# Order and pace of the weight preparation behind an attention stage

## The chip, the core and the metric

The kernel runs on one core of one Trainium2 chip. The metric is the device time of one execution in microseconds (us). Three executions of the kernel before took 1023.18, 1025.66 and 1025.5 us; the median is 1025.5 us. Engines are named as in the profile: PE is TensorE's matmul, PEld its weight load, DVE is VectorE, ACT ScalarE, POOL GpSimd, SP SyncE.

## What is computed

Three stages follow one another. All inputs are 64-bit floats; the kernel reads them as pairs of 32-bit words, and the three feed-forward weights of the first layer are turned into 32-bit floats on the chip.

```python
# attention: 4 batches, 8 heads, 576 positions, 64 wide, window of 128
scores = scale * q @ k.T ; scores = where(0 <= i - j < 128, scores - slope_h * |i - j|, -1e9)
attn   = exp(scores - max) ; attn /= sum(attn) + 1e-9 ; x = attn @ v      # x: 2304 x 512
# first layer, 512 -> 1536 -> 512
x = (silu(x @ w_gate) * (x @ w_val)) @ w_out
# second layer, 512 -> 2048 -> 512
h = x @ w_in ; out = (h * cos(h)) @ w_out2
```

## The kernel before

**Exactness.** A matrix product of the two layers is made of three matmuls: each operand is split into a high and a low half (`hi`, `lo`), and `mm3` (L79 to L82) adds high by high, high by low and low by high. Splitting an operand takes a copy (high) and a subtraction (low).

**Attention stage (L713 to L791).** A unit is one batch and one pair of heads; there are 16 units. A unit has nine items (four query blocks for each of two heads, and one item for the 64 tail rows of both heads), so the stage runs over 144 items and ten more turns to drain. The loop counter is `n`; unit u has the items 9u to 9u+8. In each turn the loop issues one step of the software pipeline for several items: scores (`do_s`), one turn later the bias (`do_bias`, DVE), two turns later the exponential (`do_exp`, ACT), then the normalising multiply (`do_norm`, POOL), transposes (`do_t`, PE), copies to high and low halves (`do_hi` ACT, `do_lo` DVE), and the product with v (`do_pv`). At fixed places in a unit the q and k of the next unit are transposed into the one buffer `pq` (`prep_t`, L426), read from there (`prep_q`, `prep_k`), and loaded for the unit after (`load_qk`, `load_v`, on SP's queue). The tail rows of q and k are transposed once in each unit, in the turn in which `n` is 4 more than a multiple of nine (L462).

**Batch 0 is different.** Units 0 to 3 (`exact(u)`, items 0 to 35) multiply plain 32-bit floats and need no halves of q and k. From item 36 on, products use halves: more instructions on ACT, DVE and POOL in each unit.

**Filler.** `filler()` (L284) issues first-layer matmuls for three of the twelve column blocks of the hidden width, in between the items, at 1.6 steps a turn (`RATE`). It can begin with a batch when that batch's attention output is complete: for batch 0 that is `release(0)`, in turn n = 45. A job is half a batch of tokens (288 columns): twelve steps with the gate weights, twelve with the value weights, and twelve with the output weights, the latter behind the next job's gate steps. When a job's third gate block has been taken out of PSUM, ACT applies Silu to all three (L236); Silu and the exponential need different tables, so ACT loads a table before and one after (1283 ns each in the trace).

**The filler's weights.** `g0_todo` (L190 to L195) lists nine pieces of 128 by 512: gate, value and output for the three blocks. `convert(..., act=True)` (L99) is a generator that prepares them. One `next(pieces)` is one step of it. A piece takes four or five steps: load of the next piece (512 KB, SP's queue) and a first ACT operation (L122); a second ACT operation (L124) and one on DVE (L125); two on DVE (L132, L133); for pieces of odd number an addition on DVE (L137), for even ones on POOL (L142). Then the high half comes from ACT (L164, even pieces) or POOL (L169, odd pieces), the low half from POOL (L157). The POOL operations go through the queue `pool_bg`, from which each turn takes about one unit of cost, and through `post`, which is emptied in the next turn. Two pieces take nine turns. A matmul step of the filler isn't issued until its piece is entered in `g0`; the generator waits in turn for older pieces.

Every engine runs its instructions in the order of issue. The list scheduler is not used (`manual_schedule`): the program order written here is the order on each queue.

Of the kernel before, what the change touches and what calls it, by code (L numbers as in the profile page):

```python
# [28 lines left out]
def kernel(  # L29
# [17 lines left out]
    NP = H // 2  # L47
# [5 lines left out]
    NI = 2 * NB + 1  # L53
# [129 lines left out]
    F0 = 3  # L183
# [5 lines left out]

    g0_todo = []  # L190
    pools0 = [wa_p, wa_p, wa2_p]
    for f in range(F0):
        g0_todo.append((("g", f), w_gate, f, True, pools0[f]))
        g0_todo.append((("v", f), w_val, f, True, pools0[f]))
    g0_todo += [(("o", f), w_out, f, False, pools0[f]) for f in range(F0)]  # L195

    def flush():
# [107 lines left out]
    def run_fill(n):  # L305
        done = 0
        while done < n and alive[0]:
            r = next(fill, None)
            if r == "wait":
                break  # L310
            if r == "end":
                alive[0] = False
                break
            done += 1
        return done
# [106 lines left out]
    def prep_t(u, nm, pool=None):  # L422
        t = nat[nm, u]
        ps = pool.tile([128, 512], F32, tag="t", name="t") if pool else ps_q.tile([128, 512], F32, tag="pq", name="pq")
        for i in range(NB):
            nc.tensor.transpose(ps[:, i * 128:(i + 1) * 128], t[:, i].rearrange("p h d -> p (h d)"), ident)  # L426
        PQ[u, nm] = ps
# [33 lines left out]
    def prep_tail_t(u, ps):  # L461
        nc.tensor.transpose(ps[:, 384:512], nat["t", u].rearrange("p h d -> p (h d)"), ident)  # L462
        PQ[u, "t"] = ps[:, 384:512]
# [30 lines left out]
    def prep_vh(u):  # L494
        if NP <= u < NP + 2:
            vhl[u % 2] = big.tile([128, NB, 4, D], F32R, tag=f"vhl{u % 2}", name=f"vhl{u % 2}")
        nc.gpsimd.tensor_scalar(v_part(u, 0), nat["v", u], 1.0, 0.0, ALU.mult, ALU.add)
# [9 lines left out]
    for u in range(U):  # L507
# [4 lines left out]
        for j in range(0, NI, 2):  # L512
            g = list(range(u * NI + j, u * NI + min(j + 2, NI)))
# [13 lines left out]
    def do_s(g):  # L527
        ps = ps_s.tile([128, 512], F32, tag="s", name="s")
        st = s_p.tile([128, 8], F32, tag="st", name="st")
        at = 0  # L530
        for m, n in enumerate(g):
            u, h, i = items[n]
            w = width(i)
            o = ps[:, at:at + w]
            at += w
            if i == NB:
                a = tail_q(u)
                c = slice(S - w, S)
                product(u, o, a, KT[u], slice(0, 128), slice(0, 128), c)
            else:  # L540
                qc = slice(i * 128, (i + 1) * 128)
                c = slice((i + 1) * 128 - w, (i + 1) * 128)
                if exact(u):
                    product(u, o, QT[u], KT[u], slice(64 * h, 64 * h + 64), qc, c)
                else:
                    product(u, o, [x[:, h] for x in QT[u]], KT[u], slice(0, 128), qc, c)
            SP[n] = o
            ST[n] = st, m

    def do_bias(n):  # L550
        u, h, i = items[n]
        w = width(i)
        p = u % NP
        e = e_p.tile([128, 256], F32, tag="e", name="e")
        st, m = ST[n]
        nc.vector.tensor_tensor_reduce(  # L556
            out=e[:, :w], in0=SP.pop(n), in1=relt if i == NB else rel[:, 256 - w:],
            scale=slope[:, p:p + 1] if i == NB else slopes[2 * p + h], scalar=3.0e38,
            op0=ALU.add, op1=ALU.min, accum_out=st[:, m:m + 1])
        E[n] = e  # L560

    def do_exp(n):
        w = width(items[n][2])
        e, (st, m) = E[n], ST[n]
        nc.scalar.activation(out=e[:, :w], in_=e[:, :w], func=AF.Exp, bias=st[:, m:m + 1], scale=-1.0,  # L565
                             accum_out=st[:, 2 + m:3 + m])

    def do_guard(g):
        st = ST[g[0]][0]
        c = len(g)  # L570
        nc.vector.tensor_scalar(st[:, 4:4 + c], st[:, 2:2 + c], 1e-9, None, ALU.add)

    def do_recip(g):
        st = ST[g[0]][0]
        c = len(g)
        nc.vector.reciprocal(out=st[:, 6:6 + c], in_=st[:, 4:4 + c])  # L576

    def do_norm(n):
        w = width(items[n][2])
        (st, m), e = ST.pop(n), E[n]  # L580
        nc.gpsimd.tensor_scalar(e[:, :w], e[:, :w], st[:, 6 + m:7 + m], 1.0, ALU.mult, ALU.mult)  # L581

    def do_t(g):
        ps = ps_t.tile([128, 512], F32, tag="t", name="t")
        at = 0
        for n in g:
            w = width(items[n][2])
            e = E.pop(n)
            for j in range((w + 127) // 128):
                c = min(j * 128, w - 128)  # L590
                nc.tensor.transpose(ps[:, at:at + 128], e[:, c:c + 128], ident)  # L591
                at += 128
        PT[g[0]] = ps[:, :at]
        TT[g[0]] = ps
# [5 lines left out]
    def do_hi(g):  # L600
        ps = PT[g[0]]
        if items[g[0]][2] == NB:
            nc.scalar.copy(out=ptt, in_=ps)
        else:
            u, h, i = items[g[0]]
            if u == NP and i == 0:
                pth[h] = big.tile([128, NB * 256 - 128], F32R, tag=f"pth{h}", name=f"pth{h}")
            nc.scalar.copy(out=pth[h][:, split_cols(g)], in_=ps)

    def do_lo(g):  # L610
        ps = PT.pop(g[0])
        if items[g[0]][2] < NB and not exact(items[g[0]][0]):
            c = split_cols(g)
            u, h, i = items[g[0]]
            if u == NP and i == 0:
                ptl[h] = big.tile([128, NB * 256 - 128], F32R, tag=f"ptl{h}", name=f"ptl{h}")
            nc.vector.tensor_tensor(out=ptl[h][:, c], in0=ps, in1=f32(pth[h][:, c]), op=ALU.subtract)
# [95 lines left out]
    CONV0, RATE = 4, 1.6  # L713
# [3 lines left out]
    for n in range(N + PVS + 1):  # L717
        due += 0.7 * RATE
        u, idx = divmod(n, NI)
        v1 = u + 1 if u + 1 < U else None  # L720

        def ended(j):
            return final.get(n - j)

        todo = list(post)
        post.clear()
        if n in first:
            do_s(first[n])
        if ended(LOW):
            do_lo(ended(LOW))  # L730
        if ended(HIGH):
            do_hi(ended(HIGH))
        for m in first.get(n - EXP, ()):
            do_exp(m)
        for m in first.get(n - 1, ()):
            do_bias(m)
        if ended(NORM):
            do_guard(ended(NORM))
        if ended(TRANS):
            do_t(ended(TRANS))  # L740
        if v1 is not None:
            if idx == TT0:
                g = ended(TRANS)
                prep_tail_t(v1, TT[g[0]] if g else ps_t.tile([128, 512], F32, tag="t", name="t"))
        if ended(NORM):
            do_recip(ended(NORM))
            for m in ended(NORM):
                do_norm(m)
        for fn in todo:
            fn()  # L750
        due -= run_fill(int(due))
        due += 0.3 * RATE
        for back in (PVS + 1, PVS):
            g = ended(back)
            if g:
                u_, h_, i_ = items[g[0]]
                if (back > PVS) == (u_ >= NP and h_ == 1 and i_ == 0):
                    for m in g:
                        do_pv(m)
        if v1 is not None:  # L760
            if idx == Q0 + 1:
                prep_q(v1)
            if idx == Q0:
                prep_t(v1, "q")
            if idx == K0:
                prep_t(v1, "k")
            if idx == K0 + 1:
                prep_k(v1)
            if idx == TT0 + 1:
                prep_tail(v1)  # L770
            if idx == max(TT0, K0) + 1:
                load_qk(u + 2)
            if idx == 7:
                load_v(u + 1)
        if u < U:
            if idx == 2:
                prep_vh(u)
            elif idx in (3, 4):
                prep_vl(u, idx - 3)
        pdue = min(pdue + 1.0, 1.0)  # L780
        while pool_bg and pdue > 0:
            cost, fn = pool_bg.popleft()
            fn()
            pdue -= cost
        if n < 8:
            t, h = qz[n // 4][n // 2 % 2], n % 2
            nc.gpsimd.memset(f32(t[64 - 64 * h:128 - 64 * h, h]), 0.0)
        if n >= CONV0:
            next(pieces, None)
        due = min(due - run_fill(int(due)), RATE)  # L790
    settle()  # L791
# [286 lines left out]
    i, tb, f = steps[0]  # L1078
# [26 lines left out]
    for k in range(K + 1):  # L1105
        if k < K:
            i, tb, f = steps[k]
# [226 lines left out]
```

## Time and profile before

| | |
|---|---|
| three timed executions | 1023.18, 1025.66, 1025.5 us; median 1025.5 |
| the profiled execution | 1027.21 us; span from the first to the last instruction 1025.4 us |
| PE busy, share of the span | 997.0 us, 97% |
| ACT, DVE, POOL busy | 648.9, 765.1, 512.6 us |
| chain that ended last, by engine | PE 88%, ACT 6% |
| mean granted clock of TensorE in the span | 0.992 |

The profiled execution is 1.7 us above the median of the timed ones. A busy PE is not always PE at its peak: the duration of a matmul of the same shape tells which of its two clocks (1.2 and 2.4 GHz) it ran at, and the column of the granted clock tells it where the recorder saw a change.

### The profile page before, as it was taken

To read this page: it belongs to the slowest core of one execution; us is meant where nothing else is said; L and a number is where in the kernel's file an instruction comes from. 1 tells how busy PE (TensorE), PEld (TensorE's weight loads), DVE (VectorE), ACT (ScalarE), POOL (GpSimd) and SP (SyncE) were. 2 spreads that over 40 slices of the span, in tenths; PEclk is the share of its full clock that TensorE was granted. 3 is DMA by queue.
4 is the path that set the end of the run, shared out by engine and by line. 5 is a ranking of instruction groups with operands and counts; after the bars stand their busy time and mean duration, and the time that the engine had idled before them with its cause. 6 is when DMAs were issued, how large, how long until landed. Compare 5 with 4: busy or idle time off the path is not lost.

```text
span 1025.4 us, 17616 instructions
## 1 busy us (share of the span) xinstructions
PE 997.0 (97%) x5796; PEld 938.7 (92%) x5796; DVE 765.1 (75%) x1600; ACT 648.9 (63%) x1438; POOL 512.6 (50%) x585
## 2 busy tenths in 40 slices
PE   7989999999999999999999999899999999999998
PEld 5778999999999999999999999798899988999986
DVE  5897797786419898998989944869866797656664
ACT  5888889887315454555545532867768777677663
POOL 5776676575315666866867840324323343222231
PEclk9989999999999999999999999999999999999999
DMA  6542333322246464755846651956667556575552
GB/s 150 135 120 48 71 85 76 80 54 66 67 159 237 124 195 127 246 162 165 266 125 212 200 175 62 312 184 202 218 199 259 167 195 195 169 260 177 184 177 82
DMA packets 145164, 163.69 MB, mean 160 GB/s; under 512 B 64689, under 2 KB 105649, under 8 KB 144817
## 3 DMA queue, kind: packets, MB, share of 16 engines
q1 hardware_dynamic: 145072, 162.57, 51.1%
q8 instruction: 46, 0.75, 0.3%
q14 instruction: 46, 0.37, 0.1%
HBM read 126.88 MB, written 35.65 MB: 158 GB/s over the span
## 4 chain that ended last, share of the span: by engine, by line
PE 88%; ACT 6%; issue 2%; DVE 2%; DMA 1%; POOL 1%; SPq 0%; POOLq 0%; ACTq 0%; DVEq 0%
PE l L80 13%; PE l L81 13%; PE l L82 13%; PE pm L80 7%; PE pm L82 7%; PE pm L81 7%; PE pm L1059 5%; PE pm L1060 5%; PE pm L1061 5%; PE pv L658 3%; PE t L591 2%; PE s L523 2%; ACT e L565 2%; PE pq L426 1%; PE s L80 1%
## 5 line engine op out<-in xcount | busy, mean ns | idle before, releaser
L1183 POOL TENSOR_TENSOR r<-r,c 128x384 f32<-128x384 f32 x96 | 104.4, 1087 | 263.6 <-ACT r L1181 174.5
L80 PE MATMUL pm<-xh,wh 128*128 128x384 f32 (+1 forms) x452 | 149.9, 332 | 0.0
L81 PE MATMUL pm<-xl,wh 128*128 128x384 f32 (+1 forms) x452 | 145.0, 321 | 0.1
L82 PE MATMUL pm<-xh,wl 128*128 128x384 f32 (+1 forms) x452 | 145.0, 321 | 0.0
L80 PE MATMUL l<-wo,hh 128*128 128x512 f32 x288 | 113.4, 394 | 0.0
L81 PE MATMUL l<-wo,hh 128*128 128x512 f32 x288 | 113.4, 394 | 0.0
L82 PE MATMUL l<-wo,hl 128*128 128x512 f32 x288 | 113.2, 393 | 0.0
L880 POOL TENSOR_TENSOR cs<-cs,st 128x512 uint32<-128x512 uint32 x56 | 80.9, 1445 | 55.1 <-DVE cs L878 47.5
L1059 PE MATMUL pm<-xh,ws 128*128 128x384 f32 x318 | 107.6, 338 | 0.0
L1061 PE MATMUL pm<-xh,ws 128*128 128x384 f32 x318 | 107.5, 338 | 0.0
L1060 PE MATMUL pm<-xl,ws 128*128 128x384 f32 x318 | 107.5, 338 | 0.0
L581 POOL TENSOR_SCALAR e<-e,st 128x256 f32<-128x256 f32 (+1 forms) x144 | 68.0, 483 | 74.8 <-DVE st L576 34.9
L1173 ACT ACTIVATE a<-c 128x384 f32<-128x384 f32 x96 | 49.8, 519 | 57.1 <-DVE c L1199 57.1
L81 PEld LDWEIGHTS pm<-xl,wh 128*128 128x128 f32 x452 | 85.1, 188 | 0.4 <-DVE xl L689 0.4
L80 PEld LDWEIGHTS pm<-xh,wh 128*128 128x128 f32 x452 | 85.0, 188 | 0.0
L82 PEld LDWEIGHTS pm<-xh,wl 128*128 128x128 f32 x452 | 84.8, 188 | 0.0
L1178 DVE SCALAR_TENSOR_TENSOR r<-a,r 128x384 f32<-128x384 f32 x96 | 76.8, 800 | 3.3
L1180 ACT ACTIVATE r<-r 128x384 f32<-128x384 f32 x96 | 50.4, 525 | 42.1 <-DVE r L1178 42.1
L565 ACT ACTIVATE e<-e,st 128x256 f32<-128x256 f32 (+1 forms) x144 | 68.0, 475 | 9.4 <-DVE st L556 8.6
L80 PE MATMUL l<-uh,wh 128*128 128x384 f32 x216 | 72.9, 337 | 0.0
L82 PE MATMUL l<-uh,wl 128*128 128x384 f32 x216 | 72.7, 337 | 0.0
L81 PE MATMUL l<-ul,wh 128*128 128x384 f32 x216 | 72.7, 337 | 0.0
(199 smaller groups left out, 2924.9 us busy)
## 6 DMA issues: line engine op xcount, KB each, us to landing
ws<-wid SPq DMA_DIRECT2D x168, 256.0 KB, 2.8
wo<-wod SPq DMA_DIRECT2D x48, 512.0 KB, 4.8
st<-in_moe_w_out_dram SPq DMA_DIRECT2D x28, 512.0 KB, 3.6
st<-in_moe_w_in_dram SPq DMA_DIRECT2D x16, 512.0 KB, 3.8
st<-in_moe_w_gate_dram SPq DMA_DIRECT2D x12, 512.0 KB, 4.5
st<-in_moe_w_val_dram SPq DMA_DIRECT2D x12, 512.0 KB, 4.2
wid<-sh SPq DMA_DIRECT2D x24, 256.0 KB, 4.1
wid<-sl SPq DMA_DIRECT2D x24, 256.0 KB, 3.6
```

What stands on the lines that cost most here:

```text
L80: nc.tensor.matmul(out=ps, lhsT=ah, rhs=bh, start=start, stop=False)
L81: nc.tensor.matmul(out=ps, lhsT=ah, rhs=bl, start=False, stop=False)
L82: nc.tensor.matmul(out=ps, lhsT=al, rhs=bh, start=False, stop=stop)
L565: nc.scalar.activation(out=e[:, :w], in_=e[:, :w], func=AF.Exp, bias=st[:, m:m + 1], scale=-1.0, accum_out=st[:, 2 + m:3 + m])
L581: nc.gpsimd.tensor_scalar(e[:, :w], e[:, :w], st[:, 6 + m:7 + m], 1.0, ALU.mult, ALU.mult)
L880: nc.gpsimd.tensor_tensor(out=ti, in0=ti, in1=st[:, :, 0], op=ALU.add)
L1059: nc.tensor.matmul(out=o, lhsT=wh, rhs=xh_, start=start and kk == 0, stop=False, skip_group_check=True)
L1060: nc.tensor.matmul(out=o, lhsT=wh, rhs=xl_, start=False, stop=False, skip_group_check=True)
L1061: nc.tensor.matmul(out=o, lhsT=wl, rhs=xh_, start=False, stop=kk == 1, skip_group_check=True)
L1178: nc.vector.scalar_tensor_tensor(out=r, in0=a, scalar=-C2, in1=r, op0=ALU.mult, op1=ALU.add)
L1180: nc.scalar.activation(out=r, in_=r, func=AF.Abs)
L1183: nc.gpsimd.tensor_tensor(out=r, in0=r, in1=h, op=ALU.mult)
```

## The change

The nine pieces are listed in another order, and for a stretch the generator is stepped half as often.

```diff
-    for f in range(F0):
-        g0_todo.append((("g", f), w_gate, f, True, pools0[f]))
-        g0_todo.append((("v", f), w_val, f, True, pools0[f]))
+    g0_todo += [(("g", f), w_gate, f, True, pools0[f]) for f in range(F0)]
+    g0_todo += [(("v", f), w_val, f, True, pools0[f]) for f in range(F0)]
     g0_todo += [(("o", f), w_out, f, False, pools0[f]) for f in range(F0)]
...
-        if n >= CONV0:
+        if n >= CONV0 and (n % 2 == 0 or n >= NP * NI):
             next(pieces, None)
```

The order was gate 0, value 0, gate 1, value 1, gate 2, value 2, output 0 to 2. It becomes gate 0 to 2, value 0 to 2, output 0 to 2. `CONV0` is 4 and `NP * NI` is 36: from turn 4 to turn 35 the generator is stepped in the even turns alone, 16 times where it was 32; from turn 36 on in each turn, as it was. No instruction is added or removed.

## Rows read from the trace of the kernel before

**Rows 1.** The page, part 1: busy us (share of span) xinstructions.

```profile
PE 997.0 (97%) x5796; PEld 938.7 (92%) x5796; DVE 765.1 (75%) x1600; ACT 648.9 (63%) x1438; POOL 512.6 (50%) x585
```

**Rows 2.** Stretches between tail transposes: length, busy (instructions) by engine, clock, DMA, GB/s.

```profile
14.00:30.61 16.61, 16.61 (x53) 11.78 (x53) 11.32 (x38) 10.00 (x30) 10.78 (x16) 1.00 0.50 138
30.61:42.16 11.55, 11.19 (x65) 8.47 (x64) 10.58 (x39) 10.87 (x34) 8.95 (x12) 1.00 0.48 123
42.16:57.99 15.83, 14.85 (x65) 10.74 (x64) 14.29 (x44) 12.60 (x37) 11.98 (x16) 0.78 0.54 149
57.99:69.44 11.45, 10.31 (x72) 8.97 (x71) 10.47 (x38) 10.96 (x32) 8.49 (x12) 1.00 0.50 114
69.44:84.32 14.88, 12.23 (x96) 11.34 (x95) 13.43 (x49) 12.75 (x39) 12.61 (x19) 1.00 0.31 78
84.32:100.78 16.46, 14.42 (x120) 14.19 (x119) 11.95 (x45) 15.76 (x41) 8.06 (x17) 1.00 0.24 55
```

**Rows 3.** Three shorter stretches, same columns (PE, PEld, DVE, ACT, POOL, clock).

```profile
50.40:57.20 6.80, 6.80 (x22) 5.32 (x22) 6.17 (x16) 4.74 (x13) 5.19 (x6) 0.52 0.32 97
8.00:29.00 21.00, 20.91 (x62) 14.55 (x62) 13.66 (x48) 12.08 (x38) 13.07 (x21) 1.00 0.57 147
116.00:124.00 8.00, 5.92 (x42) 5.54 (x40) 4.46 (x18) 7.86 (x20) 1.76 (x4) 0.89 0.07 22
```

**Rows 4.** PE's timeline, one score product of the same shape three times: start, us.

```profile
15.26 2.07 PE L523 MATMUL s<-kx,qx 64*128 64x256 f32 x4
31.68 1.13 PE L523 MATMUL s<-kx,qx 64*128 64x256 f32 x4
50.45 1.94 PE L523 MATMUL s<-kx,qx 64*128 64x256 f32 x4
```

**Rows 5.** PE's timeline, instructions that came late: in brackets the idle time before them.

```profile
48.90 0.44 PE L591 MATMUL t<-ident,e 128*128 128x128 f32 x2 [0.47 <-POOL e L581]
49.85 0.67 PE L658 MATMUL pv<-pthx,vx 128*128 128x256 f32 x2 [0.51 <-DVE xl L689]
65.35 0.67 PE L658 MATMUL pv<-pthx,vx 128*128 128x256 f32 x2 [0.72 <-DVE xl L689]
72.39 0.63 PE L426 MATMUL pq<-ident,k 128*128 128x128 f32 x4 [2.24 <-issue]
95.65 0.39 PE L658 MATMUL pv<-pth,vhl 128*128 128x256 f32 x1 [2.04 <-DVE x L671]
121.96 0.40 PE L80 MATMUL pm<-fh,wh 128*128 128x288 f32 x1 [1.47 <-ACT ye L269]
```

**Rows 6.** DVE's timeline, three operations.

```profile
46.22 1.50 DVE L132 TENSOR_SCALAR ct<-ct 128x512 uint32<-128x512 uint32 x1
49.03 0.67 DVE L689 TENSOR_TENSOR xl<-pv,xh 128x512 fp32r<-128x512 f32 x1
70.78 1.51 DVE L447 SCALAR_TENSOR_TENSOR qzl<-pq,qscale,qzh 64x512 fp32r<-64x512 f32 x2
```

**Rows 7.** POOL's timeline at the first of them.

```profile
46.16 1.27 POOL L157 TENSOR_TENSOR wl<-ct,wh 128x512 fp32r<-128x512 f32 x1
```

**Rows 8.** A piece's operations on ACT by line: ns min/median/max, first and last start.

```profile
L122 ACT ACTIVATE ct<-st x9: 664/671/702, 15.4 to 72.4; 128x512 f32<-128x512 f32 x9
L124 ACT ACTIVATE st<-st x9: 663/666/707, 16.8 to 74.3; 128x512 uint32<-128x512 uint32 x9
L164 ACT CAST wh<-ct x5: 604/609/619, 23.4 to 81.8; 128x512 fp32r<-128x512 f32 x5
```

**Rows 9.** ACT's timeline around the first Silu.

```profile
89.64 1.28 ACT L236 ACT_TABLE_LOAD   x1
94.29 0.58 ACT L667 COPY x<-pv 64x512 f32<-64x512 f32 x1
97.25 0.40 ACT L565 ACTIVATE e<-e,st 128x128 f32<-128x128 f32 x1 [0.37 <-DVE st L556]
```

**Rows 10.** SP's queue, waits ahead of the loads of gate and value: ns min/median/max.

```profile
L91 SPq EVENT_SEMAPHORE  x6: 17/28/4051, 19.9 to 39.4; - x6
```

## The prediction

> **What bounds the kernel now.** The page's first part says PE: busy 97% of the span [rows 1]. The change only touches the first tenth, so I went from the page to that stretch and cut it into units of nine items, at the tail transpose that each unit issues once; the edges are turns n = 4, 13, 22, 31, 40, 49 and 58 [rows 2]. The reader should see three things there. First, the units of batch 0 do the same work, but take 16.61, 11.55 and 15.83 us. Second, in the middle one PE is busy 11.19 of 11.55 us and ACT 10.87, DVE 10.58: three engines are nearly full at once. Third, in the next two units PE has 1.1 and 2.7 us free; ACT is busy 10.96 of 11.45 us in the first of them, DVE 13.43 of 14.88 in the second, and in the last unit ACT 15.76 of 16.46.
>
> Then PE's timeline, for the clock. The same four score matmuls take 2.07 us at 15.26, 1.13 at 31.68 and 1.94 at 50.45 [rows 4]: the first and the last run at 1.2 GHz, the middle one at 2.4. The opening stretch at the lower level is a matter of what the exact units issue: PE was busy 20.91 of 21 us in it [rows 3] (the clock column says 1.00 there; the durations decide). The second stretch, 50.4 to 57.2, has a granted clock of 0.52 [rows 3], and right before it PE stood still for 0.47 and 0.51 us [rows 5], the first time in batch 0 that two such gaps follow each other.
>
> What ends the gaps? PE waited for the normalised e from POOL, and for the low half xl, which frees the pv bank. On DVE, xl ran only at 49.03, behind a conversion step that took 1.50 us [rows 6], while POOL ran the low half of another piece from 46.16 to 47.43 [rows 7]. So what ends last here is the weight preparation, on DVE and POOL, ahead of attention's own operations.
>
> **The change part by part.** Counting steps in the code, a piece's first ACT operation is issued before in turns 5, 9, 14, 18, 23, 27, 32, 36, 41, and after in 6, 14, 24, 32, 39, 43, 48, 52, 58. Nothing is added; about three pieces move from batch 0's units to turns 39 to 65.
>
> *The order* costs nothing by itself: the filler starts at n = 45 in both, needs value 0 at n = 52 (entered at 41), value 2 at 57 (entered at 50) and output 2 at 67 (entered at 67). The last has no margin in turns, so a late piece is a risk; a turn lost holds back 1.6 steps, and these are made up later. I take 0.
>
> *Loads on SP.* The 512 KB load of the next piece moves with the first ACT operation, past q, k and v loads. SP's queue now waits up to 4.05 us for a stage buffer [rows 10], with the q and k loads behind it; at half pace the buffer is free by then. No PE gap names such a load, so I take 0 (bounds: nothing, or up to 4 us earlier loads that nobody waits for).
>
> *Third unit, 42.16 to 57.99.* It keeps one piece instead of two. I expect both gaps to go, and with them the fall of the clock, so that the unit takes what its neighbour took: 11.55 instead of 15.83, **-4.3 us**. Bounds: -1.0 (only the gaps go, 0.47 + 0.51) and -4.6 (PE busy throughout, 11.19). I take the high end's side because the neighbour did the same work at 2.4 GHz with two pieces, and a gap only of 0.36 us (11.55 less 11.19).
>
> *Turns 31 to 45.* The 2.24 us gap [rows 5] is k's transposes waiting for the bank pq, whose last readers are DVE's qzl, done at 72.29 [rows 6]; these wait for ACT, which has no room in this unit (10.96 of 11.45 us). Up to n = 39 ACT now does two first, two second operations and a high half, 4 x 0.67 + 0.61 = 3.3 us; after, one of each and the high half, 1.95 us [rows 8]. So qzl comes some 1.3 us earlier: **-1.3 us**. Bounds: 0 and -3.0 (0.72 + 2.24, both gaps gone). What is late next is PE itself.
>
> *Turns 46 to 53.* From 84.32 on ACT has 0.7 us free in the whole unit [rows 2], and what PE waits for at 95.65 (2.04 us) ends in ACT's copy at 94.29, behind the two table loads around Silu [rows 5, 9]. New ahead of that copy are L122 and L124 of piece 6 and L122 of piece 7, 2.0 us; gone is the high half of piece 8, 0.61: **+1.4 us**. Behind it, turns 53 to 64 get 3 x 0.67 + 2 x 0.61 = 3.2 us more on ACT. I take 0 for these, because ACT had caught up at 97.25, where it waited 0.37 us for new work [rows 9]; the cover is the lead that it regains while PE stands. If that cover is gone, it is 3.2. So the bounds of this part are 0 and +4.6. DVE has 4.5 us free in that unit and POOL 8.4 [rows 2]; no cost.
>
> *The longer gap.* The gap ahead of 95.65 grows to some 3.4 us. The second Silu shows what a gap may do: one of 1.47 us with another before it, and a granted clock of 0.89 over 8 us [rows 3, 5]. That is 0.22 x 8 = 1.8 us at half rate, **+0.9 us** lost. Bounds: 0, and the 3.3 us of the earlier stretch (0.48 x 6.8).
>
> Sum: -4.3 - 1.3 + 1.4 + 0.9 = -3.3 us against the profiled execution's 1027.21 us (span 1025.4), which is 1.7 above the timed median. The work behind n = 67 is unchanged and PE-bound, so the difference carries to the end: **1025.5 - 3.3 = 1022.2 us**.
>
> A rule that bears on the price: the Trainium skill, "SBUF — State Buffer", section "SBUF: two separate sides", says that DVE in some modes and GpSimd take one shared port pair as an exclusive lock, so that the loser waits for a whole instruction. The 1.50 us step, which ended 0.3 us after POOL's subtraction, agrees with it [rows 6, 7]. By that rule alone the three moved low halves could hold DVE 1.2 us each in the filler's turns, 3.6 us in all, where the sum has 0.
>
> **The rivals.**
>
> *All is hidden.* ACT absorbs the moved operations in the 2.1 us that it has free before 84.32 [rows 2], and the clock holds at the Silu gap: -4.3 - 1.3 = -5.6, **1019.9 us**. For it: PE holds up to 2.24 us of gap at 72.39 with a granted clock of 1.00 in that unit [rows 2, 5]. Against: ACT's 15.76 of 16.46 us.
>
> *The clock falls anyway.* The stretch at half rate doesn't come from the two gaps but from what batch 0's units issue, as in the opening 21 us; it stays, perhaps elsewhere. Then -1.0 - 1.3 + 1.4 + 0.9 = 0: **1025.5 us**, and the change doesn't do what it seems to do. For it: the gaps are only 1.0 us together, while 2.24 us did no harm at 72. Against: the unit before ran at full rate with PE as busy as it can be. The Trainium skill, "TensorE: Matmul & The Clock Gate", section "What's actually happening", says that the throttled state is the default and that activity releases it; read plainly, an engine that is all but busy should keep its clock, and two gaps of half a microsecond should not take it. By that rule this rival holds; the trace doesn't bear out the plain reading, since PE was busy 20.91 of 21 us at half rate.
>
> *Slower: the clock falls at the longer Silu gap and stays down.* Place: from about 90 us, in the ACT-bound turns 46 to 53. Price: half of the stretch at half rate, since PE has all the work there is from then on. With -4.3 - 1.3 + 1.4 = -4.2 before it, the kernel is slower than 0.3% (3.1 us) once that stretch is over 14.6 us; as long as the opening one (21 us) it costs 10.5: **1031.8 us**. Against: after the second Silu the fall cost under 2 us at half rate [rows 3], with the same filler matmuls.
>
> **How the numbers follow.** 0.3% of the time, 3.1 us, is about what a measurement of this kernel can tell from no change. Chances: forecast 0.46, all hidden 0.20, clock falls anyway 0.27, slower 0.07. The forecast at 1022.2 lies on the bound (1022.4); with its own spread of some 2 us I give it 0.26 faster and 0.20 same. All hidden is faster; clock falls anyway is 0.25 same, 0.02 slower. Sum: faster 0.46, same 0.45, slower 0.09. The range runs from just below the hidden case, 1019.4, to 1.1 above the third case, 1026.6; it leaves out the slower case and the ends. The forecast's own range is 1020.2 to 1024.2.
>
> **What would show it.** In the profile after: a third unit of about 11.5 us, no gaps of half a microsecond ahead of it, and score matmuls of 1.13 us at its end (step one); the k transposes of turn 41 with a gap under 1 us (step two); the gap ahead of pv at the first Silu at 3 to 4 us (step three); the granted clock around it below 1 (step four). It is wrong if a stretch at half rate is still in batch 0's units after the opening, if turns 45 to 67 take over 3 us longer than before, or if PE waits for a piece's low half.

## The result, and the profile after

The changed kernel takes 1034.26 us (median of six executions, 1032.18 to 1035.61) where the kernel before took 1025.58 beside it: a ratio of 1.0083, with a 95% interval of 1.0068 to 1.0099. It is 8.7 us slower; the forecast was 1022.2 us, faster, and its range ended at 1026.6. The profiled execution after took 1032.62 us with a span of 1030.8, so the two traces account for 5.4 us of difference, and the timed runs add some 3 us, since the profiled execution before stands above its median and the one after below it.

Part 1 of the page of the kernel after, busy us (share of span) xinstructions, stands beside [rows 1]:

```profile
PE 996.6 (97%) x5796; PEld 938.4 (91%) x5796; DVE 764.2 (74%) x1600; ACT 649.0 (63%) x1438; POOL 510.3 (50%) x585
```

Every engine has the same number of instructions as before and nearly the same busy time. So nothing was added, and the loss must be sought in when things run. The kernel after cut at the same tail transposes as [rows 2], with two more units (length, then busy (xinstructions) of PE, PEld, DVE, ACT, POOL, then granted clock, DMA share, GB/s):

```profile
13.96:29.72 15.76, 15.76 (x53) 11.20 (x53) 7.60 (x34) 8.23 (x27) 7.78 (x16) 1.00 0.39 94
29.72:41.43 11.71, 11.19 (x66) 8.47 (x64) 9.15 (x38) 9.94 (x32) 5.70 (x11) 1.00 0.48 120
41.43:52.39 10.96, 10.96 (x66) 8.45 (x64) 9.28 (x37) 10.24 (x32) 6.04 (x12) 1.00 0.54 129
52.39:63.87 11.48, 10.32 (x72) 8.92 (x71) 10.19 (x39) 10.39 (x33) 7.35 (x12) 1.00 0.51 125
63.87:81.46 17.59, 13.70 (x95) 12.88 (x94) 17.18 (x49) 14.02 (x40) 12.16 (x18) 0.90 0.47 122
81.46:101.26 19.80, 15.36 (x120) 14.25 (x118) 15.48 (x52) 18.43 (x47) 12.29 (x18) 1.00 0.33 90
101.26:119.73 18.47, 16.31 (x117) 15.27 (x115) 14.74 (x48) 12.87 (x38) 17.15 (x28) 0.91 0.22 49
119.73:138.33 18.60, 15.97 (x120) 15.59 (x119) 13.05 (x46) 16.05 (x42) 11.21 (x21) 0.91 0.31 81
```

I number these units 1 to 8. Against the kernel before, unit 1 is 0.85 us shorter, unit 3 is 4.87 shorter, and units 5, 6 and 7 are 2.71, 3.34 and 4.65 longer; the others differ by 0.3 or less, and the two units behind the eighth take what they took (units 7 and 8 before: 13.82 and 18.28 us). The sum is +5.4 us, the whole difference of the spans. So the change did what it was built to do in unit 3, and lost twice as much in units 5 to 7. There the reader sees a different engine fill each unit: DVE in unit 5 (17.18 of 17.59 us), ACT in unit 6 (18.43 of 19.80), POOL in unit 7 (17.15 of 18.47).

The seventh unit of the kernel before, then units 5 to 7 as one stretch, in the kernel before and after, same columns:

```profile
100.78:114.60 13.82, 13.82 (x116) 13.79 (x115) 12.08 (x45) 11.83 (x36) 12.26 (x24) 1.00 0.29 66
...
69.44:114.60 45.16, 40.47 (x326) 39.31 (x325) 37.46 (x137) 40.34 (x114) 32.93 (x58) 1.00 0.28 66
...
63.87:119.73 55.86, 45.37 (x327) 42.40 (x325) 47.39 (x146) 45.31 (x122) 41.61 (x62) 0.94 0.34 87
```

The stretch is 10.7 us longer. PE's own idle time in it goes from 4.69 to 10.49 us, which is 5.8. The other 4.9 are PE's busy time, 40.47 to 45.37 for the same matmuls. Most of that is the clock: it falls from 2.4 to 1.2 GHz twice, once in unit 5 and once in unit 7 (one us of each, same columns):

```profile
73.00:74.00 1.00, 1.00 (x7) 1.00 (x7) 0.98 (x3) 0.76 (x4) 0.95 (x1) 0.50 0.31 68
111.00:112.00 1.00, 1.00 (x6) 1.00 (x6) 0.50 (x4) 0.00 (x0) 1.00 (x3) 0.50 0.00 0
```

By the granted clock of the single us around them, each fall lasts 3.4 us (72.6 to 76.0 and 110.2 to 113.6); half of 6.8 us is 3.4 us lost. For the other 1.5 us the rows show no cause; 0.9 of it is in unit 6, where the recorded clock stays at 1.00.

Which waits make the idle time is seen in PE's timeline after, at the instructions that came late (start, us, what, and in brackets the idle time before it and what ended it), to be read against [rows 5]; the first line is a score product of the shape of [rows 4]:

```profile
53.46 1.13 PE L522 MATMUL s<-kx,qx 64*128 64x256 f32 x4
65.67 0.63 PE L425 MATMUL pq<-ident,k 128*128 128x128 f32 x4 [1.09 <-issue]
70.60 0.63 PE L590 MATMUL t<-ident,e 128*128 128x128 f32 x4 [1.87 <-DVE kl L484]
72.15 0.46 PE L624 MATMUL pq<-ptt,v 128*128 128x128 f32 x2 [0.93 <-DVE kl L457]
94.46 0.39 PE L657 MATMUL pv<-pth,vhl 128*128 128x256 f32 x1 [2.44 <-DVE x L670]
109.24 0.90 PE L590 MATMUL t<-ident,e 128*128 128x128 f32 x4 [2.00 <-POOL e L580]
```

The score product runs at full rate, 1.13 us; the two half-microsecond gaps of unit 3 are gone, and the k transposes wait 1.09 us instead of 2.24. In their place stand 1.87 and 0.93 us in unit 5 and 2.00 us in unit 7, and in both units the fall of the clock comes within one us behind the last of them.

Why is DVE late in unit 5? The generator has seven operations on DVE in this unit after and four before, 5.3 us against 2.8. But the operations are also slower one by one: an L570 on two columns takes 0.17 us when alone and 1.27 at 66.62, and L133 takes 0.69 or 1.64. DVE's and POOL's timelines after show why (start, us, what):

```profile
66.59 1.28 POOL L157 TENSOR_TENSOR wl<-ct,wh 128x512 fp32r<-128x512 f32 x1
66.62 1.27 DVE L570 TENSOR_SCALAR st<-st 128x2 f32<-128x2 f32 x1
...
75.28 1.45 POOL L157 TENSOR_TENSOR wl<-ct,wh 128x512 fp32r<-128x512 f32 x1
75.63 1.64 DVE L133 SCALAR_TENSOR_TENSOR ct<-st,ct 128x512 uint32<-128x512 uint32 x1
...
96.14 0.69 DVE L133 SCALAR_TENSOR_TENSOR ct<-st,ct 128x512 uint32<-128x512 uint32 x1
...
106.28 0.62 POOL L169 TENSOR_SCALAR wh<-ct 128x512 fp32r<-128x512 f32 x1
106.98 1.31 POOL L157 TENSOR_TENSOR wl<-ct,wh 128x512 fp32r<-128x512 f32 x1
107.22 1.63 DVE L133 SCALAR_TENSOR_TENSOR ct<-st,ct 128x512 uint32<-128x512 uint32 x1
108.29 1.36 POOL L580 TENSOR_SCALAR e<-e,st 128x256 f32<-128x256 f32 x2
```

In these three cases the DVE operation that meets the low half's subtraction on POOL lasts until that ends (L570) or half a us longer (L133): L133 takes 1.63 and 1.64 us there, 0.69 at 96.14 with POOL at something else. DVE and POOL work in order, so attention's operations behind them wait. In unit 5 that is `kl` on DVE, behind the held L570 and two conversion steps; the hold at 75.63 comes after both gaps of that unit. In unit 7 it is the normalising multiply on POOL (L580 at 108.29), directly behind a piece's high half (L169) and low half (L157); PE waits for it at 109.24. So unit 7's gap is made in POOL's own queue: the bias that the held L133 delays on DVE runs only later.

In unit 6 the place is ACT's queue. ACT's timeline after, around the first Silu:

```profile
87.88 1.28 ACT L235 ACT_TABLE_LOAD   x1
90.01 0.66 ACT L122 ACTIVATE ct<-st 128x512 f32<-128x512 f32 x1
90.69 1.28 ACT L564 ACT_TABLE_LOAD   x1
93.10 0.58 ACT L666 COPY x<-pv 64x512 f32<-64x512 f32 x1
```

A conversion step of 0.66 us, L122, sits between Silu and the second table load, ahead of the copy that releases PE at 94.46. The kernel before has the same copy and the same wait, 2.04 us [rows 5, 9], with no conversion step there.

### The profile page after: what moved, and what is told of

Same layout as the page of the kernel before. It is cut to its first block, busy times and chain, and to the rows that moved or that the text cites. A ratio compares the mean times of both kernels' runs of the same rounds, so it can differ in the third digit from the quotient of the medians.

```text
span 1030.8 us, 17625 instructions
## 1 busy us (share of the span) xinstructions
PE 996.6 (97%) x5796; PEld 938.4 (91%) x5796; DVE 764.2 (74%) x1600; ACT 649.0 (63%) x1438; POOL 510.3 (50%) x585
## 4 chain that ended last, share of the span: by engine, by line
PE 86%; ACT 6%; DVE 3%; issue 2%; DMA 2%; POOL 1%; SPq 0%; POOLq 0%; DVEq 0%; ACTq 0%
PE l L80 13%; PE l L81 13%; PE l L82 13%; PE pm L80 7%; PE pm L82 7%; PE pm L81 7%; PE pm L1059 5%; PE pm L1060 5%; PE pm L1058 5%; PE pv L657 2%; PE t L590 2%; PE s L522 2%; ACT e L564 1%; PE pq L425 1%; PE s L80 1%
## 5 line engine op out<-in xcount | busy, mean ns | idle before, releaser
L580 POOL TENSOR_SCALAR e<-e,st 128x256 f32<-128x256 f32 (+1 forms) x144 | 66.4, 472 | 77.5 <-DVE st L575 43.5
L1179 ACT ACTIVATE r<-r 128x384 f32<-128x384 f32 x96 | 50.4, 525 | 42.4 <-DVE r L1177 42.4
L82 PE MATMUL l<-uh,wl 128*128 128x384 f32 x216 | 72.6, 336 | 0.0
L81 PE MATMUL l<-ul,wh 128*128 128x384 f32 x216 | 72.6, 336 | 0.0
```

Of the source, the lines that this page charges most:

```text
L81: nc.tensor.matmul(out=ps, lhsT=ah, rhs=bl, start=False, stop=False)
L82: nc.tensor.matmul(out=ps, lhsT=al, rhs=bh, start=False, stop=stop)
L1179: nc.scalar.activation(out=r, in_=r, func=AF.Abs)
```

## The experiments

What is to be told apart: is it the order of the pieces or the pace; if the pace, which engine's moved operations cost the time (DVE's in front of attention's, ACT's around Silu, POOL's together with what they hold up on DVE), and is it how much work is late, or at which places of the nine-turn unit it falls? All ratios are to the kernel before on the same chip.

**The order alone.** The new list of pieces, and the generator stepped in each turn as before.

```diff
-        if n >= CONV0 and (n % 2 == 0 or n >= NP * NI):
+        if n >= CONV0:
             next(pieces, None)
```

> The new order of the nine pieces alone, at the old pace (one step in each turn from turn 4 on). Theory A (pace: late pieces load the engines of turns 36 to 65): the same pieces are done at the same turns as before, all but the last before the filler starts, so 1025.6 us within 2 us. Theory B (order: PE waits for a weight that is entered too late): the time of the changed kernel, about 1034 us.

Measured: 1024.43 us, ratio 0.9997 [0.9983, 1.0011]. The order makes no difference. Its third unit shows something more (the unit, then the two late instructions in it):

```profile
40.75:53.35 12.60, 11.61 (x66) 8.43 (x64) 12.28 (x41) 12.06 (x37) 10.90 (x14) 1.00 0.58 153
...
47.51 0.44 PE L590 MATMUL t<-ident,e 128*128 128x128 f32 x2 [0.48 <-POOL e L580]
48.45 0.67 PE L657 MATMUL pv<-pthx,vx 128*128 128x256 f32 x2 [0.51 <-DVE xl L688]
```

It carries two pieces, as before (DVE x41 and POOL x14, against x44 and x16 in [rows 2]), and yet takes 12.60 us at full clock where the profiled execution of before took 15.83. The same two gaps are there, 0.48 and 0.51 us, and the score product behind them, at 49.05, took 1.13 us. So the fall of the clock on which the first term of the forecast rested comes neither with the load alone nor with these gaps each time. Of the three traces with both gaps, two show the fall (before, and nine turns later, below) and this one doesn't; of the eight in which that unit has no gap over 0.2 us (after, and e2_pace to e8_early_pace), none does. The timed executions of the kernel before on this chip alone spread from 1021.6 to 1026.7 us.

**The pace alone.** The old list of pieces, and the half pace.

```diff
-    g0_todo += [(("g", f), w_gate, f, True, pools0[f]) for f in range(F0)]
-    g0_todo += [(("v", f), w_val, f, True, pools0[f]) for f in range(F0)]
+    for f in range(F0):
+        g0_todo.append((("g", f), w_gate, f, True, pools0[f]))
+        g0_todo.append((("v", f), w_val, f, True, pools0[f]))
```

> Half the pace alone, with the old order (gate and value in turn). Theory A: about 1034 us, as the changed kernel within 2 us, because the same work falls on the same turns. Theory B: 1025 us or below, since the order is the old one; or, if the old order makes the filler wait at half pace, above 1036 us with PE gaps ahead of the matmuls on pm that end in wh or wl.

Measured: 1032.65 us, ratio 1.0074 [1.0056, 1.0091], the whole of the change's loss within the intervals. What follows is about the pace alone.

**Each engine's share.** In three kernels the operations of the generator on one engine work on 16 of 512 columns for pieces 4 to 8 (counted from 0), those that the pace moves into turns 39 and later; these operations stay where they are in their queues. In a fourth all three are cut at once. They leave out nearly all of these pieces' arithmetic, so the filler multiplies by unfinished weights. From the fourth kernel:

```diff
+                thin = act and i >= 4
+                cw = slice(0, 16 if thin else 512)
...
-                nc.vector.tensor_scalar(ti, ti, 3, None, ALU.logical_shift_left)
...
+                nc.vector.tensor_scalar(ti[:, cw], ti[:, cw], 3, None, ALU.logical_shift_left)
```

and so on for each operation of the engine. In the cut of DVE alone some constants change too, and in the cut of ACT DVE reads the raw words. Where a half is written in part alone (the cuts of POOL, ACT and all three), it is set apart early and POOL fills it with zeros in turns 5 to 13.

> The changed kernel, in which VectorE's four operations on pieces 4 to 8 touch 16 of 512 columns, so that these pieces (value 1 and 2, output 0 to 2) hold other numbers; ScalarE and GpSimd do all they did. It takes some 12 us off DVE in turns 40 to 62. Theory A1 (DVE's queue is what ends last in the unit 63.9 to 81.5, where it is busy 17.2 of 17.6 us): 4 us or more come back, 1030 us or below, and that unit is 15 us or shorter. Theory A2 (ScalarE alone is the bound, as the prediction had it): within 1.5 us of the changed kernel, 1034 us. Theory C (the clock's falls after the gaps cost the most): whatever shortens the gaps brings the granted clock of the units 5 to 7 from 0.9 back to 1.0.

> The changed kernel, in which GpSimd's operations on pieces 4 to 8 (additions, high and low halves) touch 16 of 512 columns; the rest of these halves is zeroed by GpSimd in turns 5 to 13, in the opening stretch at the lower clock, so these pieces hold other numbers. It takes some 11 us off POOL in turns 43 to 65. Theory A3 (POOL's queue: attention's normalising multiplies wait behind the pieces' operations, and DVE's operations are held while POOL's run): 4 us or more come back, and the unit 101.3 to 119.7 is back to 14 to 15 us. Theory A2 (ScalarE alone): within 1.5 us of the changed kernel, 1034 us.

> The changed kernel, in which ScalarE's operations on pieces 4 to 8 touch 16 of 512 columns (VectorE reads the raw words in their place; the high halves of even pieces are zeroed by GpSimd in turns 5, 9 and 13; these pieces hold other numbers). It takes 5 x 1.34 + 3 x 0.61 = 8.5 us off ACT in turns 39 to 64. Theory D (each late unit has another full queue: DVE in the unit of turns 40 to 48, ACT in 49 to 57, POOL in 58 to 66): the unit 81.5 to 101.3 falls from 19.8 us to 18 or below, the one before it stays over 16.5, and 1.5 to 3.5 us of the 8.7 come back: 1030 to 1032 us. Theory A2 (ScalarE alone): 7 us or more come back, 1027 us or below. Theory C (clock): the time follows the falls, and nothing can be said before.

> The changed kernel, in which all operations on pieces 4 to 8, on ACT, DVE and POOL, touch 16 of 512 columns (their halves are zeroed by GpSimd in turns 5 to 13, in the opening stretch; these pieces hold other numbers). What is left of the change is the lighter load of turns 4 to 35. Theory D: all of the late cost goes, and the early gain stands alone; units of turns 40 to 66 take 44 us or less together (45.2 before, 55.9 after), and the time is 1018 to 1022.5 us. If the late cost were not the pieces' engine work but their loads or the order of issue, the units stay over 50 us and the time over 1028 us.

Measured, with the part of the ratio 1.0083 that each gives back:

| cut | us | ratio | gives back |
|---|---|---|---|
| DVE | 1028.25 | 1.0030 [1.0014, 1.0045] | 0.0053, 5.4 us |
| POOL | 1030.86 | 1.0050 [1.0031, 1.0069] | 0.0033, 3.4 us |
| ACT | 1030.79 | 1.0044 [1.0028, 1.0060] | 0.0039, 4.0 us |
| all three | 1023.39 | 0.9974 [0.9958, 0.9991] | 0.0109, 11.2 us |

Each engine carries a part, none of them all, and the three sum to 12.8 us against 11.2 together, which is the same within the intervals. With e2_pace's ratio as the base, which was taken beside the first two, these give back 4.5 and 2.5 us; the order of the two stays, but POOL's part is then not clear of the intervals. Two expectations fell short: POOL's cut was to give back 4 us or more, and the cut of all three was to end at 1022.5 us or below. ACT's gave back a little more than the 1.5 to 3.5 us expected. With all three cut the kernel is 2.7 us faster than before. That is not the whole gain of the early units, and not a bound on it: units 5 to 7 still take longer in its trace than before (47.55 us against 45.16), although this kernel leaves out work in unit 5 that the kernel before does.

Where each pays is seen by unit. With DVE cut, unit 5; with POOL cut, unit 7; with ACT cut, unit 6 (same columns as the units above):

```profile
64.08:78.81 14.73, 12.16 (x96) 11.33 (x95) 13.79 (x50) 14.07 (x41) 11.73 (x19) 1.00 0.60 154
```

```profile
100.77:117.15 16.38, 14.70 (x116) 13.82 (x115) 13.48 (x48) 12.59 (x37) 13.51 (x28) 1.00 0.24 55
```

```profile
81.56:99.75 18.19, 15.37 (x119) 14.26 (x118) 15.62 (x51) 15.98 (x45) 12.06 (x18) 1.00 0.32 79
```

With DVE's operations cut, unit 5 takes 14.73 us instead of 17.59, as long as before (14.88), and its clock stays at 1.00; units 6 and 7 are shorter too, by 0.95 and 1.36 us. With POOL's cut, unit 5 keeps its 17.58 us, and unit 7 falls from 18.47 to 16.38, again at full clock; in this one trace unit 8 (20.05 us at a clock of 0.83) loses that again, and the 3.4 us are a figure of the timed executions, which range from 1029.2 to 1032.7. With ACT's cut, unit 5 is 17.59 us and unit 6 falls from 19.80 to 18.19. Unit 5's excess is DVE's, some 2 us of unit 7's 4.65 are POOL's, and 1.6 of unit 6's 3.34 are ACT's; what is left of these two isn't tied to one engine. There PE's wait at the first Silu came down to 1.05 us with ACT cut; with all three cut it was 2.43 again (each kernel's PE timeline), so that wait isn't L122's alone:

```profile
92.95 0.39 PE L666 MATMUL pv<-pth,vhl 128*128 128x256 f32 x1 [1.05 <-DVE x L679]
```

```profile
91.19 0.38 PE L664 MATMUL pv<-pth,vhl 128*128 128x256 f32 x1 [2.43 <-DVE x L677]
```

With all three cut I expected units 5 to 7 to come to at most 44 us together; they took 47.55 (14.72, 18.41 and 14.42), because the middle one still needed 18.41:

```profile
79.47:97.88 18.41, 15.98 (x120) 15.73 (x119) 14.06 (x52) 16.48 (x46) 8.22 (x20) 0.91 0.30 79
```

In that unit the clock fell in this execution though hardly any conversion work was left in it, so not all of unit 6's excess belongs to the moved pieces.

The cut of POOL also tests the hold between POOL and DVE. In its unit 5 the subtraction at the place of 75.28 works on 16 columns, and the same L133 beside it takes 0.69 us instead of 1.64:

```profile
74.62 0.39 POOL L161 TENSOR_TENSOR wl<-ct,wh 128x16 fp32r<-128x16 f32 x1
74.97 0.69 DVE L133 SCALAR_TENSOR_TENSOR ct<-st,ct 128x512 uint32<-128x512 uint32 x1
```

So POOL's subtraction does lengthen L133. Unit 5 gained nothing from it, since its gaps, 1.86 and 0.92 us there, lie before. The subtraction that holds L570 ahead of those gaps belongs to piece 3, which no kernel here cuts; what that hold alone costs was not measured.

**Half pace in the third unit alone.** The pieces keep their places up to turn 21, and from the sixth on each begins four turns later than before (the last in turn 45 instead of 41).

```diff
-        if n >= CONV0 and (n % 2 == 0 or n >= NP * NI):
+        if n >= CONV0 and (n % 2 == 0 or not 22 <= n < 31):
```

> The new order, half the pace in turns 22 to 30 alone, full pace in all others: four steps are late where the change has sixteen. Theory D, with a cost that grows with the number of late steps (10.7 us for 16): some 2.7 us of cost, and an early gain of 1.6 to 4.9 us, so 1022.5 to 1026.5 us, not told from the kernel before. If any late step costs as much as all (a threshold, as with a clock that falls once), 1030 us or more.

Measured: 1027.33 us, ratio 1.0003 [0.9988, 1.0018], no change. The third unit took 11.67 us, as wanted, and unit 5 gave all of it back (its row, then the longest wait in it):

```profile
65.55:84.82 19.27, 14.65 (x95) 13.82 (x94) 17.73 (x53) 14.19 (x42) 13.69 (x21) 0.82 0.32 79
...
74.56 0.77 PE L624 MATMUL pq<-ptt,v 128*128 128x128 f32 x2 [2.94 <-DVE kl L457]
```

Four turns of delay, not quite one piece's work, are enough for a gap of 2.94 us and a clock of 0.82 in unit 5.

**The relief paid early instead of late.** Two steps a turn in turns 4 to 13, one up to 21, half pace in 22 to 30, one behind. The last pieces then come earlier than before, so that if only late work were the cost, this would be faster than both.

```diff
-        if n >= CONV0 and (n % 2 == 0 or n >= NP * NI):
+        for _ in range(0 if n < CONV0 else 2 if n < 14 else 1 if n < 22 else (n + 1) % 2 if n < 31 else 1):
             next(pieces, None)
```

> The new order, two steps in each of turns 4 to 13 (PE at the lower clock there, ACT, DVE and POOL with 5 us and more free), one in 14 to 21, half the pace in 22 to 30, full pace from 31: the third unit is as light as in the changed kernel, and the last piece is done two turns earlier than before. Theory D: the third unit takes 11 to 11.6 us, the units of turns 31 to 66 are no longer than before, and the time is 1020 to 1023 us, faster than both kernels. If the opening stretch is not free, the unit of turns 4 to 12 is longer than 16.6 us by what is added (up to 5 us), and the time is 1026 us or more.

Measured: 1030.33 us, ratio 1.0035 [1.0022, 1.0047], slower. The expectation missed in two places. Its units 1 and 5:

```profile
14.12:31.03 16.91, 14.87 (x52) 10.54 (x52) 12.74 (x40) 12.15 (x34) 11.91 (x18) 0.80 0.48 134
...
70.02:89.11 19.09, 14.89 (x96) 14.05 (x95) 15.28 (x49) 13.86 (x41) 13.47 (x21) 0.82 0.21 48
```

The opening isn't free: PE, busy throughout unit 1 before, now stands for 2.0 of 16.91 us. Unit 2 takes 14.50 us where before had 11.55. And unit 5 takes 19.09 us although no more work is left for it (three operations of the generator on DVE, where before had four). Lateness and amount don't explain that.

**The place within the unit.** If it is the place, then shifting the old sequence by a whole unit should cost less than shifting it by part of one. Three kernels with the old list and the old pace, started at turn 13 (nine later, so each step stands at the same place of a unit), at 8 (four later) and at 0 (four earlier):

```diff
-    CONV0, RATE = 4, 1.6
+    CONV0, RATE = 13, 1.6
```

> The kernel before (old order, full pace), with the first step in turn 13 in place of 4: each step nine turns, one unit, later, so at the same place of its unit. The last piece is done in turn 60, before the filler needs it in turn 67. Theory D (what counts is how much work falls on turns 36 and later): three more pieces late, 9 steps, some 6 us of cost against a gain of at most 2 in the opening units: 1029 to 1032 us, with the units of turns 40 to 57 some 5 us longer than before. Theory P (what counts is at which place of the unit a piece's steps fall; the old places are good, the new ones are not): within 2 us of the kernel before on this chip.

> The kernel before with the first step in turn 8: each step four turns later, so nearly the amount of late work of the kernel before (four steps more), at other places of the unit. Theory D: some 2.7 us more, 1028 us on a chip where the kernel before takes 1025.5. Theory P: the unit of turns 40 to 48 is over 17 us as with half pace in the third unit, and the time is 1029 us or more.

> The kernel before with the first step in turn 0: each step four turns earlier; four steps fewer fall on turns 36 and later, and the places in the unit are others than before. Theory D: the late units get shorter, by up to 2.7 us, so 1023 to 1025 us on a chip where the kernel before takes 1025.5. Theory P: some unit of turns 4 to 48 gets longer by 1 us or more, and the time is 1027 us or more.

| first step in turn | us | ratio |
|---|---|---|
| 13 | 1029.02 | 1.0025 [1.0012, 1.0039] |
| 8 | 1031.57 | 1.0060 [1.0040, 1.0079] |
| 0 | 1034.70 | 1.0089 [1.0073, 1.0106] |

Nine turns later, the latest of the three, costs least. Its unit 5 carries two pieces (before, the old sequence ends in it) and is as long as before, at full clock:

```profile
68.77:83.64 14.87, 12.22 (x95) 11.33 (x94) 14.48 (x50) 13.98 (x41) 12.61 (x17) 1.00 0.52 146
```

Four later, unit 5 has the same seven operations of the generator on DVE and hardly more work there in instructions (x54 against x50), but 3.0 us more busy time, and the gap is there, with DVE's operation held beside POOL's subtraction:

```profile
66.90:85.24 18.34, 13.71 (x95) 12.89 (x94) 17.44 (x54) 14.24 (x42) 13.42 (x20) 0.91 0.33 83
...
75.93 0.46 PE L625 MATMUL pq<-ptt,v 128*128 128x128 f32 x2 [2.94 <-DVE kl L458]
...
72.26 1.43 POOL L157 TENSOR_TENSOR wl<-ct,wh 128x512 fp32r<-128x512 f32 x1
72.60 1.63 DVE L133 SCALAR_TENSOR_TENSOR ct<-st,ct 128x512 uint32<-128x512 uint32 x1
```

Four earlier leaves the least work for units 5 to 7, and is the slowest. It pays in units 1 to 4 (17.15, 16.93, 16.67 and 15.04 us where before had 16.61, 11.55, 15.83 and 11.45). In units 2 to 4 the amount is the old one: 21 operations of the generator on DVE against 20, 12 on POOL in both. Unit 2 and its longest wait, and DVE held before it:

```profile
31.05:47.98 16.93, 14.65 (x66) 10.62 (x64) 12.81 (x42) 11.17 (x34) 10.86 (x16) 0.80 0.46 119
...
39.85 1.04 PE L658 MATMUL pv<-pthx,vx 128*128 128x256 f32 x2 [2.12 <-DVE xl L689]
...
37.20 1.69 POOL L157 TENSOR_TENSOR wl<-ct,wh 128x512 fp32r<-128x512 f32 x1
38.03 0.89 DVE L571 TENSOR_SCALAR st<-st 128x2 f32<-128x2 f32 x1
```

On the reading that late work is what costs, the nine turns should have lost 4 to 6 us and the four earlier ones nothing. Both missed, the second by its sign, though units 5 to 7 of the four earlier did get shorter, by 2.3 us. Theory P missed the nine turns too, narrowly: it allowed 2 us, the ratio gives 2.6 (1.2 to 4.0). That loss lies in units 6 and 7 (17.58 and 15.45 us; before 16.46 and 13.82), where the old sequence has no work, so late work has a price as well. What the three show together: of one and the same sequence, shifts of +9, +4 and -4 turns cost 2.5, 6 and 9 us. The place in the unit decides more than how late the work is. The plainest comparison is unit 5 with seven operations of the generator on DVE each time, in one trace each: 14.87 us nine turns later, 17.59 in the changed kernel, 18.34 four later, 19.27 with half pace in the third unit alone.

## Why the prediction was wrong

The direction was wrong: the sum was -3.3 us, the time rose by 8.7. The gains came, and the terms for the units to which the pieces went were missing or too small.

**Third unit, -4.3.** Right in its mechanism: both gaps went, the score product behind it took 1.13 us, and the unit took 10.96 us, 4.87 less. Mis-sized as a term of the timed median: it takes the half-rate stretch 50.4 to 57.2 [rows 3] as a feature of the kernel, and e1_order ran the same load, with the same two gaps, in 12.60 us without it. Against that trace the unit gains 1.6 us, and units 2 to 4 together 2.8 (34.15 us after, 36.92 in e1_order); against the trace before, which has the fall, they gain 4.7 (38.83). How often the timed executions have the fall is not known. Unit 1's 0.85 us say nothing: with the same half pace it took 15.07 us in e2_pace's trace and 16.61 in e6_thin_all's.

**Turns 31 to 45, -1.3.** The premise held: the wait at the k transposes went from 2.24 to 1.09 us. The sentence that failed is "What is late next is PE itself". What is late next is DVE: `kl`, behind a held operation and conversion steps, with gaps of 1.87 and 0.93 us, and a fall of the clock behind them. The unit grew by 2.71 us. I had ACT's queue alone in view for this unit, and [rows 2] already said that DVE was busy 13.43 of 14.88 us there.

**Turns 46 to 53, +1.4, and the operations behind it, 0.** The gap grew by 0.4, not by 1.4. But "I take 0 for these, because ACT had caught up at 97.25" failed: a single idle moment of 0.37 us was read as a lead. Unit 6 had ACT busy 18.43 of 19.80 us and grew by 3.34; cutting ACT's operations brought 4.0 us back in the timed executions (e5_thin_act), and in its trace 1.6 in unit 6. My upper bound for the part, +4.6, took this in.

**"DVE has 4.5 us free in that unit and POOL 8.4; no cost".** This is the largest error. The sentence speaks of unit 6 alone; for units 5 and 7 the sum had no term for DVE or POOL at all. DVE's moved operations cost 5.4 us and POOL's 3.4 (e3_thin_dve, e4_thin_pool). Free time as a sum over a unit is no cover for an operation that stands in an in-order queue ahead of one that PE needs now. In unit 5 that one is `kl` on DVE, in unit 7 the normalising multiply on POOL. And the two engines are tied: POOL's subtraction lengthens what DVE runs beside it.

That tie stood in the forecast. The Trainium skill, "SBUF — State Buffer", section "SBUF: two separate sides", says that DVE in some modes and GpSimd hold one port pair as an exclusive lock, so that the loser waits for a whole instruction. The rows at 66.62, 75.63 and 107.22 agree: a DVE operation of 0.17 us took 1.27, one of 0.69 took 1.64 and 1.63, each beside a POOL subtraction of 1.3 to 1.5. The two in unit 5 lost 1.1 and 0.95 us of DVE's time; the first stands ahead of a gap, the second behind both and without a price there (e4_thin_pool). The forecast worked out 3.6 us by this rule and kept 0 in its sum, though [rows 6, 7] had shown one such hold; with it the sum would have been +0.3. What it lacks of the 8.7 is in the other terms, and in the operations that wait behind the held one, which the sum didn't price at all.

**The longer Silu gap, +0.9.** Wrong place and too small. The clock fell in units 5 and 7, behind gaps of 1.87 with 0.93 and of 2.00 us, to half for 3.4 us each time; that is 3.4 us, and PE's busy time over units 5 to 7 rose by 4.9. At the Silu gap itself (2.44 us) the granted clock of the unit stayed 1.00.

**The rivals.** The slower one (0.07) came nearest in time, 1031.8, and its mechanism was not the one that ran: it had one fall at the Silu gap that lasts, where the trace has several units in which a queue is late. "The clock falls anyway" wasn't borne out for unit 3: the fall there never came without the two gaps or a longer one, though the gaps didn't always bring it. It was right that falls come elsewhere, in units 5 and 7, but behind new gaps. Of the marks that I named for a wrong forecast, the second came true: turns 45 to 67 took far over 3 us longer.

**What stays open.** No kernel that computes the whole result beats the one before. Which rule links a step's place in the unit with a gap was not worked out; another shift than the three was not tried. Why PE's matmuls run at half rate in the opening stretch was not tried either, nor why the clock falls in unit 3 in some executions and not in others. The excess of units 6 and 7 is explained only in part.

## What to carry to other kernels

Background work that is spread over in-order queues is not paid in sums of free time: for each moved instruction, look up which instruction of the critical chain stands behind it on that engine, and what the engine that it contends with runs at that moment. Moving it by a whole period of the loop keeps those neighbours, and moving it by part of one doesn't; here the whole period still cost 2.5 us, the parts 6 and 9. Before counting on a stall's removal, make sure that the stall is in more than one execution, and price each new gap on PE together with the clock that it may cost behind it.

## What the runs showed of the hardware

- A small DVE operation is held beside a POOL subtraction of 128x512 as a large one is: 128x2 elements took 1.27 us instead of 0.17, 128x512 took 1.63 instead of 0.69. The size of the held operation didn't matter, that of the subtraction did: 16 columns on DVE took 1.09 us beside a full subtraction and 0.17 later (e3_thin_dve, 66.86 and 73.87), and with the subtraction cut to 16 columns the 1.64 us became 0.69 (e4_thin_pool).
- PE's clock after a gap isn't set by the length of the gap alone: 2.24 us at 72.39 in the kernel before left the unit's granted clock at 1.00 [rows 2, 5], and 1.87 with 0.93 us in the kernel after was followed by 3.4 us at half rate. Two gaps of 0.47 and 0.51 us were followed by a fall in the kernel before, and 0.48 and 0.51 at the same place in e1_order were not.
- The same kernel's executions differ by several us: the kernel before took 1021.6 to 1026.7 us on one chip and 1021.9 to 1028.6 on another. Part of that goes with the mean granted clock: three executions at 0.998 took 1021.6 to 1022.1 us, nine at 0.996 or 0.997 took 1023.0 to 1024.3, the 48 at 0.990 to 0.995 took 1023.2 to 1028.6.
